# u's products in blocks of four token tiles, with two more x tiles kept in DRAM

## The chip, the cores and the metric

The kernel runs on one core of one Trainium2 chip. Its engines are TensorE (matmuls, in the profile PE, its weight loads PEld), VectorE (DVE), ScalarE (ACT), GpSimd (POOL) and SyncE (SP), which here only issues DMAs. The metric is the device time of one execution in microseconds, from the first to the last instruction with what lies around them.

## The reference

Two branches work on the same x (2048 tokens, 640 features) and are mixed by a gate:

```
g = sigmoid(sum(x * gate_w))                       # one value per token
a = x @ dre.T ;  b = x @ dim.T ;  y = sre @ a - sim @ b     # Fourier mixing, 2048x2048 and 640x640
q = x @ w_q ; s1 = q[..:128] @ k1.T ; s2 = q[128..] @ k2.T  # 32 heads, 16 + 16 scores each
top 2 of s1, top 2 of s2 -> 4 sums -> top 2 of them -> softmax weights gg, expert numbers e
act = gelu(x @ u[e]) ;  B = sum(gg * act * v[e])            # 256 experts
out = g * y + (1 - g) * B
```

As there are only 256 experts, the kernel computes gelu(x @ u.T) for all of them (u's products, the part that the change touches), builds the sparse matrix of weights per token, and multiplies by v.

## The kernel before, in words

Every float32 operand is split into a high and a low part (h is a rounded copy, made by ScalarE; l = f - h, by GpSimd or VectorE), and a product takes three matmuls: h by h, h by l, l by h (`mm3`, lines 143 to 145). Lines 138 and 139 are the split for every operand, so in the profile its groups are told apart by tile names.

The work is written out as one static order. The sequence transform has 128 *pieces* (`seq_piece`): for w in (re, im), for four column blocks c of 512 time steps, for 16 token tiles s of 128: five groups of three matmuls of 512 columns into banks 0 to 4 of PSUM. A column block (16 pieces) is called q; when it ends, ScalarE copies the five banks to the stage ST (line 246), VectorE multiplies by the gate (line 217) and ScalarE's queue stores the five results to DRAM (`store_piece`, line 227). A piece's own operand is loaded five pieces ahead (SP's queue) and split three pieces ahead.

`at(n, f)` hangs other work behind piece n; it is issued, in the order in which it was hung there, after that piece's matmuls:

- Pieces 0 to 29: x is loaded and split into 16 tiles X0 to X15. The query weights are folded with the keys: 32 tiles `wq` of 640 KB are loaded by SP, five in flight, and multiplied in eight groups G of 32 small matmuls (`w_part`, line 365), behind pieces 6, 9, ... 27. `make_t` and `split_w` turn the results into the score weights WH, WL and their sums TW, which lie in the place of X0 to X5.
- From piece 31, the score phase: eight pairs p of token tiles, four `score_step`s each, one behind each piece. Step 0 computes two products into bank 5, splits the sums of x (`split_sums_xT`, tiles SX), then u's products of the pair (`u_pair`, lines 720 to 731): 30 matmuls with 256 columns into bank 7, a gelu on ScalarE (line 729) and two stores on SP's queue (line 731); then ScalarE copies bank 5 to bank 7 (line 548), on which step 1 goes on. Steps 2 and 3 end the scores of the two tiles, load and split the next pair's x (tiles xh and xl, one pair each) and form its sums on VectorE (`sum_xT`, lines 437 to 440). Behind every odd pair but the last stands one piece without a step, a *filler*.
- The Pump (`bg`) hands out VectorE's picking of the top 2 (`topk`, `gates`, `weights`) and the expert matrices in small portions: each `run_bg(us)` behind a group of matmuls adds 0.95 times its time as credit, each portion issued takes its estimate from it. It also issues the copies of rows (line 697) on ScalarE by timers, 5 us apart.
- Then pieces 66 to 127 with the expert matrices (line 815) among them, and 84 steps that multiply by the hidden transform and v. Raw tiles for these steps are taken from places that have come free (`raw_tags`, `take`).

X0 to X8 have to make room in the score phase: they are stored to DRAM early (`put_x`, 9 tiles, `AWAY`), loaded again for each column block into the places of X6, X7 and X8 (`get_x`), and put back in their own places after piece 66 (N1).

All DMAs of one queue are issued in order; SP's issue waits when its operand or its place isn't ready, and what stands behind waits too.

Of the kernel before, what the change touches and what calls it, by code (L numbers as in the profile page):

```python
# [38 lines left out]
KZ = KD + 1  # L39
NSTEP = 7 * KZ  # L40
AHEAD = 5
AWAY = 9
BYPASS = 4
ACCUM_END = NT * (NC + 2) - 4

# [61 lines left out]
def gated_mix_kernel(ctx: ExitStack, tc: tile.TileContext, xT, xn, dreT, dimT, wsre, wsim, wq, kT, uT, vv, gw, out):  # L107
# [20 lines left out]
    def ps_t(shape, dt=F32):  # L128
        return bank(7, shape, dt)
# [6 lines left out]
    def split(f, h, l, eng):  # L136

        nc.scalar.activation(h, f, AF.Copy)  # L138
        eng.tensor_sub(l, f, h.bitcast(F32))  # L139
# [56 lines left out]
    def at(n, f, *args):  # L196
        then.setdefault(n, []).append(lambda: f(*args))
# [51 lines left out]
    for q in range(2 * NC):  # L249
        n = NT * (q + 1)  # L250
        at(n + (2 if q == 0 else -2 if q > 1 else -1), load_row, q)
        at(n + (7 if q == 0 else 0), gate_piece, q)
        if q in (1, 2, 3, 4):
            for d in range(KD):
                at(n + 1 + d, store_piece, q, (d,))
        else:
            at(n + (8 if q == 0 else 1), store_piece, q)


    p1_stack = ctx.enter_context(ExitStack())  # L260
    p1 = p1_stack.enter_context(tc.tile_pool(name="p1", bufs=1, reuse_waits="tile"))
    pools = [p1]

    def load_x(s):
        if s < NT:
# [4 lines left out]
    def split_x(s):  # L270

        if s < NT:
            X[s] = big.tile([P, 2, D], F32R, name="X", tag=f"X{s}")
            f = xr[s // 2][:, s % 2]
            if s:
                split(f, X[s][:, 0], X[s][:, 1], nc.vector)
                return
            psp[0] = h, l = WS[:, 0, 0], WS[:, 0, 1]
            a, b, w = slice(0, 2 * P), slice(2 * P, D), pf.pop(0)
            nc.vector.tensor_copy(X[0][:, 0, a], f[:, a])  # L280
            nc.scalar.activation(h, w, AF.Copy)
            nc.scalar.activation(X[0][:, 0, b], f[:, b], AF.Copy)
            nc.vector.tensor_sub(l, w, h.bitcast(F32))
            for c in (a, b):
                nc.vector.tensor_sub(X[0][:, 1, c], f[:, c], X[0][:, 0, c].bitcast(F32))
# [20 lines left out]


    warm = nc.const_aps.tensor(1.0, [P, 2 * P], mybir.dt.bfloat16)
    t = ps_t([P, 2 * P])
    for n in range(WARM):  # L310
        nc.tensor.matmul(t, warm[:, :P], warm, start=True, stop=True)  # L311

    split_x(0)
    load_piece(4)
# [105 lines left out]
    def split_xT(p, n):  # L420

        if p < NP:
            if not xs:
                xs.update((t, big.tile([P, 2, KD, P], F32R, name=t, tag=t)) for t in ("xh", "xl"))
            split(xf[p][:, n], xs["xh"][:, n], xs["xl"][:, n], nc.gpsimd)

    SX = {}

# [21 lines left out]
        nc.sync.dma_start(xd[s], X[s].bitcast(F32))  # L450

    def get_x(s, tag):
        X[s] = big.tile([P, 2, D], F32R, name="X", tag=f"X{tag}")
        nc.sync.dma_start(X[s].bitcast(F32), xd[s])

    for s in range(AWAY):
        at(6 + 2 * s, put_x, s)
    for s in range(3):
        at(2 * NT - 5 + s, get_x, s, 6 + s)
    for n in range(NT - 4):  # L460
        at(n, load_x, n + 4)
    for n in range(NT - 3):
# [6 lines left out]
    for G in range(NG):  # L469
        b = 6 + 3 * G  # L470
        for m in range(4 * G, 4 * G + 4):
            at(b, w_part, m)
        at(b, split_w, G)
        if G >= NG // 2:
            at(b + (4, 3, 2, 1)[G - NG // 2], make_t, G)
        for i, m in enumerate(range(4 * G + WQB, 4 * G + WQB + 4)):
            at(b + i // 2, load_wq, m)
    n = b + 2
    at(n - 8, load_xT, 0)
    for k in range(KD):  # L480
        at(n - 8 + k, load_u, k)
        at(n - 6 + k, split_u, k)
    for a in range(2):
        at(n - 3, split_xT, 0, a)
    at(n - 1, sum_xT, 0)
    assert N0 == n + 1

# [34 lines left out]
    def products(o, *terms, first=False):  # L522


        terms = [t for a, w in terms for t in zip(*a, *w)]
        for n, (ah, al, wh, wl) in enumerate(terms):
            mm3(o, ah, al, wh, wl, first and n == 0, n == len(terms) - 1, True)
            run_bg(0.68)

    def x_part(n, k0, k1):  # L530
        return [[xs[t][:, n, k] for k in range(k0, k1)] for t in ("xh", "xl")]

    def s_part(n):
        return [[t[:, k * P:(k + 1) * P] for k in range(2)] for t in SX[n]]
# [9 lines left out]
    def score_step(p, a):  # L544


        i0, i1 = 2 * p, 2 * p + 1
        copy = lambda o, f: nc.scalar.activation(o, f, AF.Copy)  # L548
        if a == 0:
            AB["A"] = bank(5)  # L550
            products(AB["A"], (x_part(0, 0, 2), w_part2(0, 2, 0)), first=True)
            split_sums_xT(p)
            u_pair(p)
            AB["Z"] = bank(7)
            copy(AB["Z"], AB["A"])
        elif a == 1:
            products(AB["Z"], (x_part(0, 2, 4), w_part2(2, 4, 0)), (x_part(0, 4, 5), w_part2(4, 5, 0)))
            new_sc(i0)
            copy(sc_half(i0, 0), AB["Z"])
            AB["Y"] = bank(6)  # L560
            products(AB["Y"], (s_part(1), t_part(1)), first=True)
            AB["Z"] = bank(7)
            copy(AB["Z"], AB["Y"])
            load_xT(p + 1)
        elif a == 2:
            products(AB["A"], (s_part(2), t_part(2)))
            copy(sc_half(i0, 1), AB["A"])
            products(AB["Z"], (s_part(4), w_part2(2, 4, 1)), (x_part(0, 4, 5), w_part2(4, 5, 1)))
            nc.vector.tensor_add(sc_half(i0, 1), sc_half(i0, 1), AB["Z"])
            bg.credit -= 0.75  # L570
            picks(i0, scs.pop(i0))
            products(AB["A"], (s_part(3), t_part(3)))
            new_sc(i1)
            copy(sc_half(i1, 1), AB["A"])
            split_xT(p + 1, 0)
        else:
            products(AB["Y"], (x_part(1, 4, 5), w_part2(4, 5, 1)))
            nc.vector.tensor_add(sc_half(i1, 1), sc_half(i1, 1), AB["Y"])
            products(AB["A"], (x_part(1, 2, 4), t_part(4)), (x_part(1, 4, 5), w_part2(4, 5, 0)))
            copy(sc_half(i1, 0), AB["A"])  # L580
            bg.credit -= 0.75
            picks(i1, scs.pop(i1))
            split_xT(p + 1, 1)
            sum_xT(p + 1)
# [132 lines left out]
        if i % NB == NB - 1:  # L717
            bg.add(gates(i // NB))

    def u_pair(p):  # L720
        xh, xl = xs["xh"], xs["xl"]
        ps = bank(7, (P, 2, 2 * P))
        for n in range(2):
            c = slice(n * P, (n + 1) * P)
            for k in range(KD):
                mm3(ps[:, n, :], UH[:, k, c], UL[:, k, c], xh[:, :, k, :], xl[:, :, k, :], k == 0 and n == 0, k == KD - 1, True)
            run_bg(1.8)
        act = p2.tile([P, 2, 2 * P], F32, name="act")
        nc.scalar.activation(act, ps, AF.Gelu_apprx_tanh)
        for n in range(2):  # L730
            nc.sync.dma_start(actd[n][:, 2 * p * P:2 * (p + 1) * P], act[:, n])

    for p in range(NP):
        n = N0 + 4 * p + p // 2
        for a in range(4):
            at(n + 1 + a, score_step, p, a)
    N1 = n + 5
# [3 lines left out]
            at(n - (3 if s > 2 else 5), get_x, s, 6 + s % 3)  # L741
    for s in range(3, AWAY):
        at(N1 - 5 + s, get_x, s, s)
    for s in range(3):
        at(N1 + 6 + 3 * s, get_x, s, s)

# [116 lines left out]
            draw.pop(m)  # L863

    for m in range(2):
        at(N1 + 4 + 2 * m, load_dd, m)
    for m in range(KD):
        for a in range(2):
            at(N1 + 6 + 5 * m + 2 * a, split_dd, m, a)
# [44 lines left out]
    def split_sums(k):  # L914
        if k == KD:
            f = p3.tile([P, 4 * TC], F32R, name="ts", tag="hot0")
            TS[8] = f[:, :2 * D]
            raw_free.append(f[:, 2 * D:2 * D + TC].bitcast(F32))
            raw_tags.extend((("xf", 2), ("X9", 2)))
        for n in () if k == KD else [k] + ([5 + k // 2] if k % 2 == 0 else []):  # L920
            TS[n] = big.tile([P, 2 * D], F32R, name="ts", tag=f"X{(1, 3, 4, 5, 6, 0, 2, 7)[n]}")
        t = T["t"]
        t1, t5, t3, t6 = (t[:, n * 2 * P:(n + 1) * 2 * P] for n in range(4))
        for n, f in enumerate((t1, t3, t5, t6, t[:, 8 * P:])):
            split(f, t_sum(k, n, 0), t_sum(k, n, 1), nc.gpsimd if n < 2 else nc.vector)
        bg.credit -= 1.0

    def load_v():
        T[KD] = big.tile([P, 2, D], F32, name="dt", tag="X9")
        nc.sync.dma_start(T[KD], vv.rearrange("k p d -> p k d"))  # L930

    def split_v():
# [13 lines left out]
    at(NPC + 14, store_gates, 1)  # L946


    fresh, raw_free = deque(), deque()
    raw_tags = [("X8", 2)] + [("wf", 1)] * 4 + [("X10", 2), ("wf", 1)] + [(f"X{s}", 2) for s in range(11, 16)]  # L950
    raw, sp = {}, {}

    def take(key):
# [305 lines left out]
```

## Time and profile before

| | before |
|---|---|
| median of 3 runs | 753.86 us (752.98 to 754.19) |
| the profiled execution | 753.44 us, span 751.7 us |
| TensorE busy | 746.7 us, 4045 matmuls |
| VectorE busy | 587.4 us |
| ScalarE busy | 361.7 us |
| GpSimd busy | 346.6 us |
| DMA | 165.89 MB, mean 221 GB/s |

A line of the timeline gives the start (us from the span's beginning), the length (us), the engine, the source line, the instruction, what it writes <- what it reads, the shapes where there are any, and how many are merged; in brackets the time that the engine stood idle before it and what ended that. "ACTq" and "SPq" are DMA issues on the engine's queue. A line of the windows gives a stretch, its length, the busy time of PE, PEld, DVE, ACT and POOL with their numbers of instructions, the granted clock, the DMA engines' busy share and GB/s. A line of the waits names who waited for whom: us in total, how often, the longest. A line of the chain that ended last gives start, length and what ran.

### The profile page before, as it was taken

What the parts mean: (1) busy time and instruction counts of PE and PEld (TensorE: products, weight loads), DVE (VectorE), ACT (ScalarE), POOL (GpSimd) and SP (SyncE); (2) the same over time, 40 slices, a digit from 0 to 9 for tenths busy, and PEclk for the clock granted to TensorE, in tenths of its full rate; (3) what the DMA queues carried; (4) which work ended last, traced back from release to release, by engine and by line L of the source; (5) the groups of instructions that cost most, each with busy time, mean ns of one, the idle gap of its engine ahead of it and who ended that gap; (6) DMA issues with size and microseconds to landing.
All of it is one profiled execution on the core that took longest, in us unless ns stands there. A gap on an engine that the chain in (4) does not pass through costs nothing.

```text
span 751.7 us, 11366 instructions
## 1 busy us (share of the span) xinstructions
PE 746.7 (99%) x4045; PEld 610.7 (81%) x4045; DVE 587.4 (78%) x741; ACT 361.7 (48%) x660; POOL 346.6 (46%) x286
## 2 busy tenths in 40 slices
PE   9999999999999999999999999999999999999998
PEld 7777777888888888888888888888888888888887
DVE  6864088278999999998999888979999983357651
ACT  4334134534345835553734687633555653443451
POOL 5533225342424424334345445643356793487253
PEclk9999999999999999999999999999999999999999
DMA  9999999478366786663496856388766689775301
GB/s 334 378 388 356 342 381 345 132 191 278 57 174 149 184 273 164 159 167 118 121 376 210 175 146 203 116 255 291 264 225 209 218 261 335 228 233 182 112 29 71
DMA packets 84490, 165.89 MB, mean 221 GB/s; under 512 B 16081, under 2 KB 23377, under 8 KB 84177
## 3 DMA queue, kind: packets, MB, share of 16 engines
q1 hardware_dynamic: 70960, 140.89, 55.5%
q0 software_dynamic: 5472, 9.96, 8.6%
q10 hardware_dynamic: 8000, 14.31, 5.2%
q8 instruction: 32, 0.52, 0.3%
q14 instruction: 26, 0.20, 0.1%
HBM read 132.46 MB, written 31.08 MB: 218 GB/s over the span
## 4 chain that ended last, share of the span: by engine, by line
PE 96%; DMA 2%; DVE 2%; issue 0%; SPq 0%; ACT 0%
PE b L143 30%; PE b L144 30%; PE b L145 30%; PE b L239 2%; PE b L365 2%; DMA wq<-in_wq 2%; PE b L815 1%; PE b L311 1%; DVE ST L217 1%; DVE WU L139 0%; DVE tw L139 0%; DVE wp L371 0%; ACT WU L138 0%; DVE tt L397 0%; DVE tt L396 0%
## 5 line engine op out<-in xcount | busy, mean ns | idle before, releaser
L143 PE MATMUL b<-WS,X 128*128 128x512 f32 x620 | 243.5, 393 | 0.0
L144 PE MATMUL b<-WS,X 128*128 128x512 f32 x620 | 241.5, 389 | 0.0
L145 PE MATMUL b<-WS,X 128*128 128x512 f32 x620 | 241.3, 389 | 0.0
L139 POOL TENSOR_TENSOR WS<-wf,WS 128x512 fp32r<-128x512 f32 x89 | 135.9, 1532 | 162.8 <-ACT WS L138 157.9
L143 PEld LDWEIGHTS b<-WS,X 128*128 128x128 f32 x620 | 116.4, 188 | 28.0 <-issue 4.1
L145 PEld LDWEIGHTS b<-WS,X 128*128 128x128 f32 x620 | 116.4, 188 | 24.5
L144 PEld LDWEIGHTS b<-WS,X 128*128 128x128 f32 x620 | 116.4, 188 | 23.3
L138 ACT ACTIVATE WS<-wf 128x512 fp32r<-128x512 f32 x89 | 55.7, 629 | 76.9 <-PE b L145 32.1
L803 DVE TENSOR_TENSOR hot<-rows,wtab 128x1024 f16<-128x1024 f16 x64 | 62.7, 1005 | 0.7 <-PE b L815 0.6
L139 POOL TENSOR_TENSOR WS<-ra,WS 128x512 fp32r<-128x512 f32 x39 | 55.1, 1426 | 15.3 <-ACT WS L138 13.2
L139 POOL TENSOR_TENSOR xl<-xf,xh 128x640 fp32r<-128x640 f32 x16 | 28.2, 1767 | 69.3 <-ACT xh L138 62.9
L138 ACT ACTIVATE WS<-ra 128x512 fp32r<-128x512 f32 x55 | 34.5, 631 | 50.9 <-PE b L145 36.0
L548 ACT ACTIVATE sc<-b 128x512 f32<-128x512 f32 x32 | 19.2, 600 | 80.7 <-PE b L145 80.7
L191 POOL DMA_DIRECT2D WS<-in_wsre x30 | 26.4, 880 | 68.0 <-ACT WS L189 66.6
L773 ACT ACTIVATE b<-b,mask 128x128 f32<-128x128 f32 x128 | 43.0, 342 | 13.5 <-PE b L815 10.4
L139 POOL TENSOR_TENSOR WP<-ra,WP 128x512 fp32r<-128x512 f32 x18 | 26.4, 1482 | 43.2 <-ACT WP L138 43.1
L598 DVE TENSOR_TENSOR eq<-sc,mm 128x1024 f16<-128x1024 f32 x32 | 41.4, 1293 | 0.9
L605 DVE TENSOR_REDUCE tied<-eq 128x64 f32<-128x1024 f16 x32 | 39.0, 1219 | 0.9
L596 DVE TENSOR_REDUCE mm<-sc 128x64 f32<-128x1024 f32 x32 | 38.8, 1212 | 0.3
L217 DVE SCALAR_TENSOR_TENSOR ST<-ST,grow 128x512 f32<-128x512 f32 x40 | 31.4, 846 | 0.6 <-ACT ST L246 0.6
L143 PE MATMUL b<-WU,xh 128*128 128x512 f32 x80 | 31.2, 391 | 0.0
L145 PE MATMUL b<-WU,xl 128*128 128x512 f32 x80 | 31.1, 389 | 0.0
(203 smaller groups left out, 1468.8 us busy)
## 6 DMA issues: line engine op xcount, KB each, us to landing
wq<-in_wq SPq DMA_DIRECT2D x32, 640.0 KB, 7.1
X<-xd SPq DMA_DIRECT2D x30, 640.0 KB, 6.6
wf<-in_wsim SPq DMA_DIRECT2D x64, 256.0 KB, 4.8
wf<-in_wsre SPq DMA_DIRECT2D x63, 256.0 KB, 6.5
ra<-pd SPq DMA_DIRECT2D x47, 256.0 KB, 3.7
pd<-ST ACTq DMA_DIRECT2D x35, 256.0 KB, 5.2
WS<-in_wsre POOLq DMA_DIRECT2D x30, 256.0 KB, 5.3
xd<-X SPq DMA_DIRECT2D x9, 640.0 KB, 9.4
```

What stands on the lines that cost most here:

```text
L138: nc.scalar.activation(h, f, AF.Copy)
L139: eng.tensor_sub(l, f, h.bitcast(F32))
L143: nc.tensor.matmul(o, wh, ah, start=first, stop=False, skip_group_check=more)
L144: nc.tensor.matmul(o, wh, al, start=False, stop=False, skip_group_check=more)
L145: nc.tensor.matmul(o, wl, ah, start=False, stop=last, skip_group_check=more)
L191: nc.gpsimd.dma_start(l, (wsre, wsim)[w][c, s], accum_op=OP.add)
L217: nc.vector.scalar_tensor_tensor(f, f, -1.0 if w else 1.0, g, op0=OP.mult, op1=OP.mult)
L596: nc.vector.tensor_reduce(m, sc, op=OP.max, axis=AX.X)
L598: nc.vector.tensor_tensor(eq, sc, m[:, :, None].to_broadcast([P, HH, E]), op=OP.is_equal)
L605: nc.vector.tensor_reduce(tied[:, s, ib, :], eq, op=OP.add, axis=AX.X)
L773: nc.scalar.activation(f[:, :, n], f[:, :, n], AF.Copy, scale=mask4[:, n:n + 1])
L803: nc.vector.tensor_tensor(o, a, b, op=op)
```

## The change

- **u's products.** `u_pairs` replaces `u_pair`. It runs in step 0 of odd pairs only and takes both pairs, so 512 columns: 15 matmuls into bank 7, 15 into bank 6, a gelu on each, and one store of 256 KB behind each gelu, now on ScalarE's queue. The first half's gelu is issued before bank 5's copy to bank 7, the second half's after it. The pump is told 0.68 us per group of three, where it was told 1.8 us per 15.
- **Places.** To keep x of two pairs, xh and xl become tiles of two pairs each. xh takes the places of X9 and X10, xl those of X11 and X12; each two places are now one allocation (`place`, `TWIN`). So X9 and X10 are stored to DRAM too (`AWAY` 11), behind piece 25, and loaded on demand like X0 to X8; X11 and X12 are copied by ScalarE to the old places of xh and xl behind pieces 16 and 17 (`move_x`), and back behind piece 66. The first split of x goes from piece 26 to 27.
- **Stores.** The five stores of q = 0 go from piece 24 to piece 28.
- **Fillers.** They stand behind pairs 0, 2 and 4 instead of 1, 3 and 5.
- **After the score phase.** The loads of the hidden transform for `split_dd` start one and two pieces later; v's tile and the raw tiles are placed anew on the joined places. The last of the 19 warm-up matmuls fills the other half of its bank.

```diff
-AWAY = 9
+AWAY = 11
@@ store_piece
-            at(n + (8 if q == 0 else 1), store_piece, q)
+            at(n + (12 if q == 0 else 1), store_piece, q)
@@ new
+    TWIN = {}
+    def place(tag):
+        if tag in (9, 11):
+            TWIN[tag] = big.tile([P, 2, 2, D], F32R, name="X", tag=f"X{tag}")
+        if tag in (9, 10, 11, 12):
+            return TWIN[tag - (tag + 1) % 2][:, (tag + 1) % 2]
+        return big.tile([P, 2, D], F32R, name="X", tag=f"X{tag}" if isinstance(tag, int) else tag)
+
+    def move_x(s, tag):
+        old, X[s] = X[s], place(tag)
+        nc.scalar.activation(X[s], old.bitcast(F32), AF.Copy)
@@ split_xT
-                xs.update((t, big.tile([P, 2, KD, P], F32R, name=t, tag=t)) for t in ("xh", "xl"))
-            split(xf[p][:, n], xs["xh"][:, n], xs["xl"][:, n], nc.gpsimd)
+                xs.update((t, big.tile([P, 2, 2, KD, P], F32R, name=t, tag=tag)) for t, tag in (("xh", "X9"), ("xl", "X11")))
+            split(xf[p][:, n], xs["xh"][:, p % 2, n], xs["xl"][:, p % 2, n], nc.gpsimd)
@@ schedule of pieces 0 to 29
-    for s in range(AWAY):
+    for s in range(9):
         at(6 + 2 * s, put_x, s)
+    for s, tag in ((11, "xh"), (12, "xl")):
+        at(s + 5, move_x, s, tag)
+    for s in range(9, AWAY):
+        at(b - 2, put_x, s)
-        at(n - 3, split_xT, 0, a)
+        at(n - 2, split_xT, 0, a)
@@ score_step, a == 0
             split_sums_xT(p)
-            u_pair(p)
+            act = u_pairs(p // 2) if p % 2 else lambda: None
             AB["Z"] = bank(7)
             copy(AB["Z"], AB["A"])
+            act()
@@ u's products
-    def u_pair(p):
+    def u_pairs(c):
         xh, xl = xs["xh"], xs["xl"]
-        ps = bank(7, (P, 2, 2 * P))
+        def act(n, ps):
+            f = p2.tile([P, TC], F32, name="act")
+            nc.scalar.activation(f, ps, AF.Gelu_apprx_tanh)
+            nc.scalar.dma_start(actd[n][:, c * TC:(c + 1) * TC], f)
         for n in range(2):
-            c = slice(n * P, (n + 1) * P)
+            e = slice(n * P, (n + 1) * P)
+            ps = bank(7 - n)
             for k in range(KD):
-                mm3(ps[:, n, :], UH[:, k, c], UL[:, k, c], xh[:, :, k, :], xl[:, :, k, :], k == 0 and n == 0, k == KD - 1, True)
-            run_bg(1.8)
-        act = p2.tile([P, 2, 2 * P], F32, name="act")
-        nc.scalar.activation(act, ps, AF.Gelu_apprx_tanh)
-        for n in range(2):
-            nc.sync.dma_start(actd[n][:, 2 * p * P:2 * (p + 1) * P], act[:, n])
+                mm3(ps, UH[:, k, e], UL[:, k, e], xh[:, :, :, k, :], xl[:, :, :, k, :], k == 0, k == KD - 1)
+                run_bg(0.68)
+            if n == 0:
+                act(n, ps)
+        return lambda: act(1, ps)
 
     for p in range(NP):
-        n = N0 + 4 * p + p // 2
+        n = N0 + 4 * p + min((p + 1) // 2, 3)
@@ after the score phase
+    for s in (11, 12):
+        at(N1, move_x, s, s)
-        at(N1 + 4 + 2 * m, load_dd, m)
+        at(N1 + 5 + 3 * m, load_dd, m)
```

More of the change, by code (lines that the diff above doesn't have):

```diff
@@ L272, in split_x @@
         if s < NT:
-            X[s] = big.tile([P, 2, D], F32R, name="X", tag=f"X{s}")
+            X[s] = place(s)
             f = xr[s // 2][:, s % 2]
@@ L308, in gated_mix_kernel @@
     warm = nc.const_aps.tensor(1.0, [P, 2 * P], mybir.dt.bfloat16)
-    t = ps_t([P, 2 * P])
+    t = ps_t([P, TC])
     for n in range(WARM):
-        nc.tensor.matmul(t, warm[:, :P], warm, start=True, stop=True)
+        c = slice(0, 2 * P) if n < WARM - 1 else slice(2 * P, TC)
+        nc.tensor.matmul(t[:, c], warm[:, :P], warm, start=n < WARM - 1, stop=True, skip_group_check=n == WARM - 1)
     split_x(0)
@@ L452, in get_x @@
     def get_x(s, tag):
-        X[s] = big.tile([P, 2, D], F32R, name="X", tag=f"X{tag}")
+        X[s] = place(tag)
         nc.sync.dma_start(X[s].bitcast(F32), xd[s])
-    for s in range(AWAY):
+    for s in range(9):
         at(6 + 2 * s, put_x, s)
@@ L528, in products, with x_part @@
             run_bg(0.68)
-    def x_part(n, k0, k1):
-        return [[xs[t][:, n, k] for k in range(k0, k1)] for t in ("xh", "xl")]
+    def x_part(p, n, k0, k1):
+        return [[xs[t][:, p % 2, n, k] for k in range(k0, k1)] for t in ("xh", "xl")]
     def s_part(n):
@@ L550, in score_step @@
             AB["A"] = bank(5)
-            products(AB["A"], (x_part(0, 0, 2), w_part2(0, 2, 0)), first=True)
+            products(AB["A"], (x_part(p, 0, 0, 2), w_part2(0, 2, 0)), first=True)
             split_sums_xT(p)
-            u_pair(p)
+            act = u_pairs(p // 2) if p % 2 else lambda: None
             AB["Z"] = bank(7)
             copy(AB["Z"], AB["A"])
+            act()
         elif a == 1:
-            products(AB["Z"], (x_part(0, 2, 4), w_part2(2, 4, 0)), (x_part(0, 4, 5), w_part2(4, 5, 0)))
+            products(AB["Z"], (x_part(p, 0, 2, 4), w_part2(2, 4, 0)), (x_part(p, 0, 4, 5), w_part2(4, 5, 0)))
             new_sc(i0)
@@ L567, in score_step @@
             copy(sc_half(i0, 1), AB["A"])
-            products(AB["Z"], (s_part(4), w_part2(2, 4, 1)), (x_part(0, 4, 5), w_part2(4, 5, 1)))
+            products(AB["Z"], (s_part(4), w_part2(2, 4, 1)), (x_part(p, 0, 4, 5), w_part2(4, 5, 1)))
             nc.vector.tensor_add(sc_half(i0, 1), sc_half(i0, 1), AB["Z"])
@@ L576, in score_step @@
         else:
-            products(AB["Y"], (x_part(1, 4, 5), w_part2(4, 5, 1)))
+            products(AB["Y"], (x_part(p, 1, 4, 5), w_part2(4, 5, 1)))
             nc.vector.tensor_add(sc_half(i1, 1), sc_half(i1, 1), AB["Y"])
-            products(AB["A"], (x_part(1, 2, 4), t_part(4)), (x_part(1, 4, 5), w_part2(4, 5, 0)))
+            products(AB["A"], (x_part(p, 1, 2, 4), t_part(4)), (x_part(p, 1, 4, 5), w_part2(4, 5, 0)))
             copy(sc_half(i1, 0), AB["A"])
@@ L917, in split_sums @@
             TS[8] = f[:, :2 * D]
-            raw_free.append(f[:, 2 * D:2 * D + TC].bitcast(F32))
-            raw_tags.extend((("xf", 2), ("X9", 2)))
+            raw_free.extend(LENT[0][:, a * TC:(a + 1) * TC] for a in range(2))
+            raw_tags.append(("xf", 2))
         for n in () if k == KD else [k] + ([5 + k // 2] if k % 2 == 0 else []):
@@ L928, in load_v @@
     def load_v():
-        T[KD] = big.tile([P, 2, D], F32, name="dt", tag="X9")
+        f = big.tile([P, 2, 2, D], F32, name="dt", tag="X9")
+        T[KD], f = f[:, 0], f[:, 1].rearrange("p k d -> p (k d)")
+        fresh.extend(f[:, a * TC:(a + 1) * TC] for a in range(2))
+        LENT.append(T[KD].rearrange("p k d -> p (k d)"))
         nc.sync.dma_start(T[KD], vv.rearrange("k p d -> p k d"))
@@ L946, in gated_mix_kernel @@
     at(NPC + 14, store_gates, 1)
-    fresh, raw_free = deque(), deque()
-    raw_tags = [("X8", 2)] + [("wf", 1)] * 4 + [("X10", 2), ("wf", 1)] + [(f"X{s}", 2) for s in range(11, 16)]
+    LENT, fresh, raw_free = [], deque(), deque()
+    raw_tags = [("X8", 2)] + [("wf", 1)] * 5 + [("X11", 5)] + [(f"X{s}", 2) for s in range(13, 16)]
     raw, sp = {}, {}
```

## The prediction

> **What bounds the kernel now.** I read the page first (busy time, granted clock, the chain that ended last), then TensorE's timeline, then the timelines of ScalarE and VectorE where a pair of token tiles ends.
>
> ```profile
> PE 746.7 (99%) x4045; PEld 610.7 (81%) x4045; DVE 587.4 (78%) x741; ACT 361.7 (48%) x660; POOL 346.6 (46%) x286
> PEclk9999999999999999999999999999999999999999
> PE 96%; DMA 2%; DVE 2%; issue 0%; SPq 0%; ACT 0%
> ```
>
> TensorE is the bound from end to end, at its full granted clock. So time can only be won by fewer or cheaper matmuls, or in the few gaps between them. A matmul's busy time doesn't tell its price, because successive matmuls overlap; the distance from start to start does. TensorE's timeline around u's products of pair 0, and at the kernel's end, where the moving operand is a plain row of 256:
>
> ```profile
> 136.95 0.28 PE L143 MATMUL b<-xh,WU 128*128 128x256 f32 x1
> 140.54 0.40 PE L143 MATMUL b<-WS,X 128*128 128x512 f32 x1
> 143.97 0.39 PE L143 MATMUL b<-WU,xh 128*128 128x512 f32 x1
> 147.37 0.39 PE L143 MATMUL b<-WS,X 128*128 128x512 f32 x1
> 150.77 0.39 PE L143 MATMUL b<-tw 128*128 128x512 f32 x1
> ...
> 743.88 0.28 PE L143 MATMUL b<-WP,ts 128*128 128x256 f32 x1
> 748.07 0.28 PE L145 MATMUL b<-WS,ts 128*128 128x256 f32 x1
> ```
>
> The 30 matmuls of u take 140.54 - 136.95 = 3.59 us, 119.7 ns each. Fifteen matmuls of 512 columns (147.37 to 150.77) take 3.40 us, 226.7 ns each. Twice 119.7 is 239.4: halving the width costs 12.7 ns a matmul. That isn't the broken-up operand of u (two stretches of 128): at the end 35 matmuls on plain rows take 4.19 us, 119.7 ns again.
>
> **The change part by part.** (1) *u in 512 columns.* Eight blocks of 30 matmuls become four of 30: 240 x 119.7 = 28.72 us goes, 120 x 226.7 = 27.20 us comes: -1.52. The piece right behind a narrow block takes 143.97 - 140.54 = 3.43 us instead of 3.40; behind wide matmuls it has no cause to: 8 x 0.03 = -0.24. Bounds: four stretches of 128 might cost something two don't, then the gain is 0; more than 1.76 there isn't.
>
> [...]
>
> (2) *The stores of q = 0 (the first column block's results) go from piece 24 to piece 28; x tiles 9 and 10 are stored at piece 25.* TensorE's only real gaps are at the keys' products (line 365). The chain in order of time, TensorE's timeline, ScalarE's and SP's queue:
>
> ```profile
> 80.21 2.29 PE b L365 x32
> ```
> ```profile
> 105.56 1.82 PE L365 MATMUL b<-wq,kp 128*32 128x320 f32 x24
> ...
> 108.28 0.50 PE L143 MATMUL b<-WS,X 128*128 128x512 f32 x1
> ...
> 118.72 1.82 PE L365 MATMUL b<-wq,kp 128*32 128x320 f32 x24
> 121.17 0.74 PE L365 MATMUL b<-wq,kp 128*32 128x320 f32 x8 [0.63 <-DMA wq<-in_wq]
> 121.85 0.50 PE L143 MATMUL b<-WS,X 128*128 128x512 f32 x1
> ```
> ```profile
> 104.64 3.93 ACTq L227 DMA_DIRECT2D pd<-ST  x5
> ```
> ```profile
> 114.24 0.63 SPq L356 DMA_DIRECT2D wq<-in_wq  x1
> ```
>
> A group of 32 takes 2.29 us; the last two take 108.28 - 105.56 = 2.72 and 121.85 - 118.72 = 3.13: 0.43 + 0.84 = 1.27 us of waiting for wq. Just ahead of the second wait ScalarE's queue issues 5 x 256 KB of stores. At piece 28 they come when the last wq tile has been used. The two stores of 640 KB that take their place stand behind wq's last load (114.24) in SP's queue. Bounds 0 and 1.27; I take -1.05, all of the second wait and half of the first, whose tile was loading before the stores began. What the new places cost: the stores block ScalarE for up to 3.93 us at piece 28 instead. Behind them stand make_t's splits and pair 0's sums; pair 0's copy into bank 7 moves to about 138.2 (four splits of 128x256, then the copy), wanted at 135.59 + 1.36 + 3.40 = 140.4: hidden, 2.2 us to spare, and 1.7 us is lost if the full block comes on top. The first split of x now also waits for tiles 9 and 10 to be stored; pieces are split three ahead, some 10 us.
>
> (3) *Steps and fillers.* In an even pair u's 3.59 us goes and a filler piece of 3.40 follows the pair; in an odd pair u takes 6.80 and the filler behind it goes. Pair to pair that is 29.3 and 32.7 us where 29.5 and 32.9 were, so VectorE's share of work per pair stays (its pacing counts 27.2 us for u where it counted 28.8):
>
> ```profile
> 227.40:260.20 32.80, 32.80 (x160) 27.78 (x159) 30.55 (x34) 22.57 (x33) 12.22 (x12) 1.00 0.71 167
> 260.20:289.70 29.50, 29.50 (x146) 25.01 (x145) 28.85 (x45) 13.77 (x24) 10.70 (x11) 1.00 0.84 254
> 378.40:420.00 41.60, 41.60 (x185) 34.47 (x184) 40.71 (x53) 17.62 (x24) 21.14 (x15) 1.00 0.90 295
> ```
>
> But between an odd pair's end and the next even pair's second step the cover shrinks. That step's first matmul needs line 548's copy into bank 7, which stands on ScalarE behind the splits of x's sums. From the pair's last matmul TensorE has one piece, six matmuls, one piece: 3.40 + 1.36 + 3.40 = **8.16 us**, where it had 15.2. The chain now, by the first matmul after pairs 1, 3, 5 and 6, VectorE's first sum (line 437), and ScalarE:
>
> ```profile
> 191.11 0.39 PE L143 MATMUL b<-WS,X 128*128 128x512 f32 x1
> 253.43 0.39 PE L143 MATMUL b<-WS,X 128*128 128x512 f32 x1
> 315.75 0.39 PE L143 MATMUL b<-WS,X 128*128 128x512 f32 x1
> 348.61 0.39 PE L143 MATMUL b<-WS,X 128*128 128x512 f32 x1
> ...
> 360.52 0.50 PE L143 MATMUL b<-WU,xh 128*128 128x512 f32 x1
> ```
> ```profile
> 194.22 0.43 DVE L437 TENSOR_TENSOR xf<-xf 128x256 f32<-128x256 f32 x1 [1.03 <-POOL xl L139]
> 256.92 0.43 DVE L437 TENSOR_TENSOR xf<-xf 128x256 f32<-128x256 f32 x1 [1.41 <-POOL xl L139]
> 318.85 0.43 DVE L437 TENSOR_TENSOR xf<-xf 128x256 f32<-128x256 f32 x1 [1.02 <-POOL xl L139]
> 354.91 0.42 DVE L437 TENSOR_TENSOR xf<-xf 128x256 f32<-128x256 f32 x1
> ```
> ```profile
> 196.52 0.71 ACT L138 ACTIVATE h<-xf 128x256 fp32r<-128x256 f32 x2
> 259.25 1.94 ACT L697 ACTIVATE rows<-rt 128x384 f16<-128x384 f16 x1
> 261.61 0.71 ACT L138 ACTIVATE h<-xf 128x256 fp32r<-128x256 f32 x2
> 322.90 0.72 ACT L138 ACTIVATE h<-xf 128x256 fp32r<-128x256 f32 x2
> 323.51 1.97 ACT L697 ACTIVATE rows<-rt 128x384 f16<-128x384 f16 x1
> 357.22 0.72 ACT L138 ACTIVATE h<-xf 128x256 fp32r<-128x256 f32 x2 [0.46 <-DVE xf L440]
> 359.89 0.58 ACT L548 ACTIVATE b<-b 128x512 f32<-128x512 f32 x1
> ```
>
> With 0.6 us for the copy, it would end at 197.83, 262.9 and 324.2 for pairs 2, 4 and 6: 6.7, 9.5 and 8.5 us after the pair's end. Pair 2 fits. Pairs 4 and 6 are late by 1.3 and 0.3 as ScalarE stands, since one or two copies of rows (line 697) go first. These come at 5 us intervals by the pump's clock, and the splits are now issued 3.4 us of TensorE's time sooner, so the fourth copy of rows falls behind them. Without it pair 4 would be about 2.5 us earlier. Bounds 0 and 1.6; I take +0.3. In odd pairs the cover grows to 18 us (15 for pair 7), and pair 7's present wait goes: its second step starts at 360.52, right behind the copy (359.89 + 0.58), 360.52 - 348.61 = 11.91 us after the pair's end where 3.40 + 1.36 + 3.59 + 3.43 = 11.78 were due, and a further 0.16 is lost in its first matmuls: -0.29.
>
> (4) *Hidden.* Six more loads of x (36 for 30) and two more stores, and u's results on ScalarE's queue:
>
> ```profile
> X<-xd SPq DMA_DIRECT2D x30, 640.0 KB, 6.6
> ```
> ```profile
> SPq L731 <- ACT act L729: 86.8, 8, 21.3
> ```
>
> The tightest stretch is 378 to 420, at 295 GB/s; two loads more make it (12.3 + 1.3 MB) / 41.6 us = 327. Loads go out three pieces (10.2 us) ahead and land in 6.6; cost 0, some 2 us if they slip by half. SP's queue no longer stands 86.8 us behind the gelu; its transfers weren't late for TensorE, so that's worth 0. The gelu's store on ScalarE delays what follows by 0.4 us, in odd pairs only. The four copies that move tiles 11 and 12 take some 1.3 us each (my estimate, from 0.63 us for 512 columns and 0.74 for 640), at pieces 16, 17 and 66 where ScalarE is idle over half the time. Near piece 122 v's load must wait for one x tile more, 3.4 us; it goes out after that already.
>
> **Sum:** 753.44 (the profiled execution: span 751.7) - 1.52 - 0.24 - 1.05 - 0.29 + 0.30 = 750.64, that is -2.80. The median of the runs is 0.42 above the profiled one; from it the sum would be 751.06. I put 751.0.
>
> **The rivals.**
> - *wq's waits stay.* Its loads queue behind x's tiles and pieces too, and the first wait began with a load issued ahead of the stores. Then 753.86 - 1.75 = about 752.1. For it: the DMA engines are full here with or without the stores. Against: 1.3 MB less ahead of the last load is over 3 us, more than the 0.84 that it lacked. Chance 0.17.
> - *The copies of rows stay ahead of bank 7's copy* in pairs 4 and 6, the fourth too (323.51 + 1.97 + 0.6 = 326.1, 10.3 after the pair): 1.3 + 2.2 = 3.5 us, the gain is gone: 753.9. Chance 0.13.
> - *Slower: VectorE arrives late in the even pairs.* In pair 7 it didn't wait for anything before the sums; it was behind, and began 354.91 - 348.61 = 6.3 us after the pair's end, against 3.1, 3.5 and 3.1 in pairs 2, 4 and 6. From its start to the copy's end it takes 3.6 us, so from 4.6 us on TensorE waits; at 6.3 it's 1.7 us in each of the three pairs, and 753.86 - 3.1 + 5.1 = 755.9. It turns the balance from a mean lateness of 1.0 us. Against: gates and weights, which make VectorE late, still come in even pairs and hit odd ones. Chance 0.10.
> - *Four stretches of 128 cost what two matmuls did:* u brings 0, 752.5. Chance 0.05, as the end's plain rows show no price for two.
>
> **How the numbers follow.** The forecast has the remaining 0.55: 751.0, its own range 750.1 to 752.2 (wq 0 to 1.27, bank 7 0 to 1.6). A measurement here can tell about 0.2%, 1.5 us. Faster by more (below 752.35): all of the forecast, 0.12 of the first rival, 0.03 of the rest: 0.70. Slower: 0.10. Within: 0.20. The range for 8 in 10 goes from 749.7 (everything won, 753.86 - 3.32, less the 0.9 us by which the lowest run stood under the median) to 753.9.
>
> **What would show it.** Right: u's matmuls 226 to 228 ns apart, four blocks of 6.8 us; the last two groups of line 365 at 2.3 us; no wait of TensorE at the second step of pairs 2, 4 and 6. Wrong: 240 ns there; 3.1 us for the last group; line 548's copy ending within 0.1 us of that step's first matmul, with line 697 or a late line 437 ahead of it; or a new wait of TensorE on an X tile after 380 us or on VectorE's hot tiles near the end.

## The result, and the profile after

The changed kernel takes 758.49 us, the median of six runs (756.62 to 760.36); the kernel before, on the same chip, 753.51 (752.22 to 754.30). The ratio is 1.0065, with a 95% interval of 1.0046 to 1.0085: **slower by 5 us**, where 751.0 was forecast. The profiled execution took 757.09 us (span 755.2), 3.65 more than the one of before.

The page of the changed kernel, its engines and the chain that ended last:

```profile
PE 745.7 (99%) x3925; PEld 603.5 (80%) x3925; DVE 588.6 (78%) x741; ACT 365.2 (48%) x664; POOL 344.3 (46%) x286
PE 67%; issue 12%; DVE 10%; POOL 6%; DMA 3%; SPq 1%; ACT 0%; POOLq 0%; ACTq 0%; DVEq 0%
```

There are 120 matmuls fewer, as meant. But the chain, 96% TensorE before, is 67% TensorE now: somewhere TensorE waits for others. Its timeline, at the keys' products and then in pair 3 and pair 7, shows the gains and the losses side by side:

```profile
105.06 2.36 PE L380 MATMUL b<-wq,kp 128*32 128x320 f32 x32
117.77 2.36 PE L380 MATMUL b<-wq,kp 128*32 128x320 f32 x32
...
226.27 0.39 PE L143 MATMUL b<-xh,WU 128*128 128x512 f32 x1
233.07 0.39 PE L143 MATMUL b<-WS,X 128*128 128x512 f32 x1
236.25 0.39 PE L145 MATMUL b<-WS,X 128*128 128x512 f32 x1
237.64 0.50 PE L143 MATMUL b<-WU,xh 128*128 128x512 f32 x1 [1.00 <-ACT b L567]
247.97 0.39 PE L145 MATMUL b<-WU,xl 128*128 128x512 f32 x1
250.48 0.50 PE L143 MATMUL b<-tw,h 128*128 128x512 f32 x1 [2.12 <-ACT sc L567]
...
350.61 0.39 PE L143 MATMUL b<-xh,WU 128*128 128x512 f32 x1
360.59 0.39 PE L145 MATMUL b<-WS,X 128*128 128x512 f32 x1
362.88 0.50 PE L143 MATMUL b<-WU,xh 128*128 128x512 f32 x1 [1.91 <-ACT b L567]
```

What was won: both groups of the keys' products (line 380 now) run as 32 matmuls in one row, with no wait between 24 and 8 of them; u's block takes 233.07 - 226.27 = 6.80 us for 30 matmuls, 226.7 ns each. What was lost: between two starts that are normally 0.23 us apart lie 1.39, 2.51 and 2.29 us, so TensorE stands for 1.16, 2.28 and 2.06 us. With the slower matmuls right behind each stop, the pieces and steps there take 4.0 us more than their matmuls need in pair 3, and 2.8 in pair 7. In pairs 1 and 5 TensorE has no such stop.

All three stops end with a copy by ScalarE (line 567; it was 548). ScalarE's timeline in pairs 3, 5 and 7, and SP's queue in pairs 3 and 7 (its last row is pair 7's):

```profile
229.87 0.60 ACT L747 ACTIVATE act<-b 128x512 f32<-128x512 f32 x1 [1.21 <-PE b L145]
236.62 0.34 ACTq L748 DMA_DIRECT2D actd<-act  x1
237.01 0.58 ACT L567 ACTIVATE b<-b 128x512 f32<-128x512 f32 x1 [6.53 <-DMA X<-xd]
239.25 0.60 ACT L747 ACTIVATE act<-b 128x512 f32<-128x512 f32 x1 [1.66 <-DMA actd<-act]
241.82 0.33 ACTq L748 DMA_DIRECT2D actd<-act  x1
242.19 0.63 ACT L188 ACTIVATE WS<-wf 128x512 fp32r<-128x512 f32 x1 [2.34 <-DMA xf<-in_xT]
...
248.08 1.93 ACT L717 ACTIVATE rows<-rt 128x384 f16<-128x384 f16 x1
249.47 0.96 ACT L567 ACTIVATE sc<-b 128x512 f32<-128x512 f32 x1
...
299.13 0.60 ACT L747 ACTIVATE act<-b 128x512 f32<-128x512 f32 x1 [1.82 <-PE b L145]
305.67 0.33 ACTq L748 DMA_DIRECT2D actd<-act  x1
...
354.75 0.72 ACT L138 ACTIVATE h<-xf 128x256 fp32r<-128x256 f32 x2 [0.46 <-DVE xf L455]
356.78 0.60 ACT L747 ACTIVATE act<-b 128x512 f32<-128x512 f32 x1
361.85 0.35 ACTq L748 DMA_DIRECT2D actd<-act  x1
362.25 0.58 ACT L567 ACTIVATE b<-b 128x512 f32<-128x512 f32 x1 [4.87 <-DMA rt<-gs]
```
```profile
232.20 0.57 SPq L469 DMA_DIRECT2D X<-xd  x1
...
237.52 1.00 SPq L433 DMA_DIRECT2D xf<-in_xT  x2
...
359.58 1.09 SPq L712 DMA_TRANSPOSE rt<-gs  x1
```

The gelu of pair 3 ends at 230.47, but its store goes out only at 236.62: ScalarE stands still for 6.15 us, and with it the copy that TensorE's next step needs. In pair 7 it's 4.47 us (357.38 to 361.85). The brackets name what ended the wait, and it's nothing that has to do with the store: **an X tile, a load of x (xf) and a transpose of the experts' weights (rt<-gs), all three on SP's queue.** How long those took from issue to landing, in the view of the DMA issues around each:

```profile
X<-xd SPq DMA_DIRECT2D x1, 640.0 KB, 4.3
...
xf<-in_xT SPq DMA_DIRECT2D x1, 320.0 KB, 4.2
...
rt<-gs SPq DMA_TRANSPOSE x1, 2.2
```

232.20 + 4.3 = 236.5, 237.52 + 4.2 = 241.7 and 359.58 + 2.2 = 361.8: ScalarE's three stores go out at 236.62, 241.82 and 361.85, each within 0.1 us of such a landing. In pair 5 the second store is held too, for 5.94 us (299.73 to 305.67), until an X tile has landed; no stop of TensorE follows there.

That 4.47 us cost more in pair 7 than 6.15 in pair 3 has to do with VectorE. In pair 7 its sums of x come late, ScalarE's splits wait for them (the bracket at 354.75), and the gelu ends 6.77 us after u's block begins (350.61), where in pair 3 it ends after 4.20. So ScalarE had 6.15 - 1.16 = 5.0 us of cover in pair 3 and 4.47 - 2.06 = 2.4 in pair 7.

Why these? The trace records which semaphore each DMA raises (in 16 steps, the last of them the landing) and for which one an engine waits. In the changed kernel's trace SP's 459 DMAs and ScalarE's 60 share eight semaphores (100, 102 to 105 and 108 to 110), and GpSimd's 38 have eight others (111 to 118). In the list in which the built program has the DMAs of both queues, the eight follow each other in one order that repeats over all 519. So a DMA's semaphore was last used by the DMA **eight places before it in that list**, and of the 511 that have one there, none went out in this trace before that one had landed. Counted in the list: eight places before the first store of pair 3 stands the load of X, eight before the second a half of xf, eight before the first store of pair 7 the transpose of gs.

The trace shows the wait itself: just ahead of the stores at 236.62, 241.82, 305.67 and 361.85 ScalarE waits for the very semaphore that the store then raises (100, 109, 100 and 100), and the DMA that used it before had landed at 236.54 (X), 241.74 (xf), 305.60 (X) and 361.77 (gs). In eight of the traces, those of the two kernels and of e1, e3, e4, e7, e8 and e9 below, none of 4088 DMAs of the two queues (511 in each) went out before its semaphore's previous user had landed.

In the experiments this is **theory O** (the order decides). In a first form, **theory L**, I had only that a store on ScalarE's queue waits for loads of SP's. The rivals: **S**, VectorE's sums are late; **B**, the single buffer `act` makes the second gelu wait; **B2**, that single buffer on ScalarE's queue; **P**, a gate row loaded one piece later is the cure; **Q**, the queue hurts only with the new tiling.

### The profile page after: what moved, and what is told of

The parts are those of the page before. It is cut to its first block, busy times and chain, and to the rows that moved or that the text cites. A ratio compares the mean times of both kernels' runs of the same rounds, so it can differ in the third digit from the quotient of the medians.

```text
span 755.2 us, 11144 instructions
## 1 busy us (share of the span) xinstructions
PE 745.7 (99%) x3925; PEld 603.5 (80%) x3925; DVE 588.6 (78%) x741; ACT 365.2 (48%) x664; POOL 344.3 (46%) x286
## 4 chain that ended last, share of the span: by engine, by line
PE 67%; issue 12%; DVE 10%; POOL 6%; DMA 3%; SPq 1%; ACT 0%; POOLq 0%; ACTq 0%; DVEq 0%
PE b L143 21%; PE b L144 20%; PE b L145 20%; PE b L380 2%; PE b L239 2%; POOL xl L139 2%; POOL WS L191 2%; DVE eq L618 1%; DVE tied L625 1%; POOL WS L139 1%; PE b L844 1%; DVE mm L616 1%; DMA WS<-in_wsim 1%; DMA actd<-act 1%; DVE eq L623 1%
## 5 line engine op out<-in xcount | busy, mean ns | idle before, releaser
L139 POOL TENSOR_TENSOR xl<-xf,xh 128x640 fp32r<-128x640 f32 x16 | 26.5, 1660 | 70.7 <-ACT xh L138 70.7
L832 DVE TENSOR_TENSOR hot<-rows,wtab 128x1024 f16<-128x1024 f16 x64 | 54.4, 876 | 2.5 <-PE b L844 2.5
L139 POOL TENSOR_TENSOR WS<-ra,WS 128x512 fp32r<-128x512 f32 x33 | 47.4, 1447 | 14.8 <-ACT WS L138 14.6
L138 ACT ACTIVATE WS<-ra 128x512 fp32r<-128x512 f32 x47 | 29.4, 631 | 42.8 <-PE b L145 29.9
L618 DVE TENSOR_TENSOR eq<-sc,mm 128x1024 f16<-128x1024 f32 x32 | 43.9, 1371 | 0.9
L217 DVE SCALAR_TENSOR_TENSOR ST<-ST,grow 128x512 f32<-128x512 f32 x40 | 33.2, 893 | 1.5 <-DMA grow<-gdr 1.5
L139 POOL TENSOR_TENSOR WP<-ra,WP 128x512 fp32r<-128x512 f32 x13 | 19.2, 1489 | 31.0 <-ACT WP L138 30.9
L832 DVE TENSOR_TENSOR hot<-hot,rows 128x1024 f16<-128x1024 f16 x32 | 33.1, 1036 | 0.0
```

Of the source, the lines that this page charges most:

```text
L217: nc.vector.scalar_tensor_tensor(f, f, -1.0 if w else 1.0, g, op0=OP.mult, op1=OP.mult)
L618: nc.vector.tensor_tensor(eq, sc, m[:, :, None].to_broadcast([P, HH, E]), op=OP.is_equal)
L832: nc.vector.tensor_tensor(o, a, b, op=op)
```

## The experiments

### The stores on another queue, and a second buffer

Four versions of the changed kernel; e1 has one of the two edits, e3 the other, e2 and e5 both.

```diff
 e1: the stores on SP's queue
-            nc.scalar.dma_start(actd[n][:, c * TC:(c + 1) * TC], f)
+            nc.sync.dma_start(actd[n][:, c * TC:(c + 1) * TC], f)
 e3: a second buffer for the second gelu, in the place of a gate row
-            f = p2.tile([P, TC], F32, name="act")
+            f = p2.tile([P, TC], F32, name="act", tag=("act", "grow")[n])
 ... which is loaded one piece later for it
-        at(n + (2 if q == 0 else -2 if q > 1 else -1), load_row, q)
+        at(n + (2 if q == 0 else -2 if q > 1 and q != 3 else -1), load_row, q)
 e2: both edits, nc.sync        e5: both edits, nc.gpsimd
```

> The changed kernel, but u's results are stored on SP's queue again; one buffer for the gelu's result, as in the change. Theory L (the store on ScalarE's queue has to wait until an SP load issued some DMAs before it has landed, and that load stands behind the loads of rows which wait for VectorE's weights; so ScalarE stands still 6.1 us in pair 3 and 4.4 us in pair 7): ScalarE is free for bank 7's copy, so the first stall of each of these pairs goes (1.2 + 0.4 and 2.1 + 0.6 us), but the second gelu still waits for the first result's store to land, now behind the same loads on SP's queue, which keeps ScalarE late in pair 3: 752 to 754. Rival S (VectorE's sums come too late in pairs 3 and 7): as the changed kernel, 757 to 759. Rival B (only the one buffer matters): 756 to 758.

> The changed kernel, with u's results stored on SP's queue and the second half's gelu in a buffer of its own (the gate row's place; the gate row of q = 3 is loaded one piece later). Theory L: nothing holds ScalarE back in pairs 3 and 7 any more, TensorE has no gap over 0.5 us between 130 and 380, and the predicted gains stay: 750 to 751.5. Rival S: 757 to 759. Rival B: 750 to 751.5.

> The changed kernel with two buffers for the gelu, the stores still on ScalarE's queue. Theory L: the first store still waits for the SP load, so bank 7's copy comes as late as in the changed kernel (TensorE waits 1.2 us in pair 3 and 2.1 us in pair 7); the second gelu is then no longer held up, which wins 1 to 2 us: 755 to 757. Rival S: 757 to 759. Rival B: 750 to 751.5.

> The changed kernel with two buffers, the stores on GpSimd's queue, whose DMAs don't take turns with SP's and ScalarE's. Theory L: no stall of ScalarE; a store takes GpSimd about 0.9 us (line 191's row), four pairs times two; GpSimd is idle there: 750 to 752. Rival S: 757 to 759. Rival B: 750 to 752.

Beside a kernel before of 754.25 us: e1 750.45 (ratio 0.9950, interval 0.9937 to 0.9964), e2 750.55 (0.9952, 0.9939 to 0.9964), e3 750.20 (0.9947, 0.9934 to 0.9959), e5 750.15 (0.9948, 0.9936 to 0.9961). All four are faster than both kernels, by some 4 us and some 8 us, and TensorE has no stop over 0.4 us anywhere in the score phase. S falls as a cause by itself, as VectorE's sums are as late in all of them as in the changed kernel: in pair 7 the last one begins 3.2 us after u's block. B falls in the same way: e1 has a single buffer and loses nothing. That is also better than its expected 752 to 754, as its second gelu isn't held up in pair 3. But e3 was a miss for theory L: the stores are still on ScalarE's queue, and nothing is lost. ScalarE's timeline of e3:

```profile
230.95 0.60 ACT L747 ACTIVATE act<-b 128x512 f32<-128x512 f32 x1 [1.20 <-PE b L145]
231.58 0.33 ACTq L748 DMA_DIRECT2D actd<-act  x1
```

The store goes out 0.03 us after its gelu. In the built list of e3 the first store of pair 3 stands six places earlier, ahead of the gate row, three transposes and xf's two loads; eight places before it is then a raw tile that had landed (at 211.22). Only in pair 5 is e3's second store held, for 5.9 us and without a stop of TensorE, as in the changed kernel. That made theory O of theory L: not the queue alone, but the place in the order. But e3 also has a second buffer and a later gate row, either of which might be the cure, so the next runs change one thing each.

### The place in the order, with queue and buffer as they are

```diff
 e7: the gates' weights are let in later; the transposes of gs and rp follow them
-        bg.after(4.0, lambda: bg.q[0].appendleft(weights(b, c, rp, gs)))
+        bg.after(4.0 if b == NT // NB - 1 else 10.0, lambda: ...)
 e8: the later gate row of e3 alone
-        at(n + (2 if q == 0 else -2 if q > 1 else -1), load_row, q)
+        at(n + (2 if q == 0 else -2 if q > 1 and q != 3 else -1), load_row, q)
 e9: the first step of those transposes later
-            bg.space(lambda a=a: step(a), 5.0 if a else 16.0 if b == NT // NB - 1 else 8.0)
+            bg.space(lambda a=a: step(a), 5.0 if a else 16.0 if b == NT // NB - 1 else 16.0)
```

> The changed kernel, its one buffer act and ScalarE's queue kept; only the gates' weights (L689 to L697 of the changed kernel) are let in 10 us instead of 4 us of background time after their exponential, in all batches but the last. In the order of the program the stores of pairs 3 and 7 then stand ahead of rt<-gs, so the DMA that used a store's completion semaphore before is one that landed long before. Theory O (a store on ScalarE's queue waits until the DMA eight places before it in the program's order, SP's and ScalarE's counted together, has landed): ScalarE issues both stores within 0.5 us of their gelu, and no step of pairs 3 and 7 has a gap of TensorE over 0.5 us behind them: 750 to 752 us. Rival B2 (one buffer on ScalarE's queue is the cause, wherever the store stands): the second gelu is held as before, 756 to 759 us. Rival P (e3 was cured because the gate row of q=3 came later): 756 to 759 us. Against theory O would be a late X tile that comes out of SP's queue behind rt<-gs, 6 us later than now: up to 2 us more.

> The changed kernel with the other half of e3 alone: the gate row of q=3 is loaded one piece later, the buffer act stays single and the stores stay on ScalarE's queue. In the program's order the four odd pairs' stores stand where they stood. Theory O: nothing changes, the first store of pair 3 goes out some 6 us after its gelu, that of pair 7 some 5 us after: 757 to 760 us. Rival P (the later gate row was what cured e3): 750 to 752 us.

> The changed kernel; only the first step of the gate rows (L712's transposes) is spaced by 16.0 instead of 8.0. By the program's order the store of pair 7 then has an X tile of long before eight places ahead, the store of pair 3 the same rt<-gs that follows VectorE's weights (231.03 us in the changed kernel), with no X tile between. Theory O, a dose: no hold in pair 7 (2.8 us of TensorE's time back), in pair 3 a hold of 2 to 4 us in place of 5.1 us, 1 to 3 us of gaps in place of 4.0: 752.5 to 755.5 us. Rival B2: as the changed kernel, 756.5 to 759.5. Rival P: as the changed kernel too.

Beside a kernel before of 753.68 us: e7 750.78 us (ratio 0.9962, interval 0.9948 to 0.9977), e8 762.29 (1.0109, 1.0089 to 1.0129), e9 751.52 (0.9965, 0.9953 to 0.9977). **Theory O holds, B2 and P fall.** ScalarE's timelines, of e7 and e8 and e9 in this order:

```profile
231.19 0.60 ACT L747 ACTIVATE act<-b 128x512 f32<-128x512 f32 x1 [1.21 <-PE b L145]
231.81 0.33 ACTq L748 DMA_DIRECT2D actd<-act  x1
```
```profile
357.26 0.60 ACT L747 ACTIVATE act<-b 128x512 f32<-128x512 f32 x1
365.00 0.33 ACTq L748 DMA_DIRECT2D actd<-act  x1
365.37 0.58 ACT L567 ACTIVATE b<-b 128x512 f32<-128x512 f32 x1 [7.51 <-DMA grow<-gdr]
```
```profile
230.81 0.60 ACT L747 ACTIVATE act<-b 128x512 f32<-128x512 f32 x1 [1.21 <-PE b L145]
235.77 0.33 ACTq L748 DMA_DIRECT2D actd<-act  x1
236.15 0.58 ACT L567 ACTIVATE b<-b 128x512 f32<-128x512 f32 x1 [4.74 <-DMA rt<-gs]
```

In e7 the DMA eight places before, a raw tile's load, had landed at 211.26, and the store goes out at once. In e9 it's rt<-gs, as counted beforehand, and the store waits for it. In e8 pair 7 waits longer than expected, 7.1 us where "some 5" stood: the gate row had moved behind rt<-gs in the list and become the eighth itself. The time, 762.3, missed the expected 757 to 760 mostly by that: of the 5.3 us between the two profiled executions some 3.6 are pair 7's, and 1.3 are a longer wait of TensorE for an operand's load at 428 us, which I have not traced. Six different kinds of DMA have thus ended the wait of a store (an X tile, xf, gs, a gate row, and in e4 below rp and a raw tile), each the one that the count names.

e9 came out better than the 752.5 to 755.5 expected: a hold of 4.36 us (231.41 to 235.77) in pair 3 stopped TensorE nowhere in the score phase. That fits the 5.0 us of cover that 6.15 us and a stop of 1.16 gave for this pair.

### The queue alone, in the kernel before

```diff
 e4: the kernel before
-            nc.sync.dma_start(actd[n][:, 2 * p * P:2 * (p + 1) * P], act[:, n])
+            nc.scalar.dma_start(actd[n][:, 2 * p * P:2 * (p + 1) * P], act[:, n])
```

> The kernel before with one thing changed: its u stores (L731) go out on ScalarE's queue. In its program's order the DMA eight places before the first store of pair 3 is rt<-rp of the second row step, which SP issued at 235.93 and which landed at 242.58 in the trace of before, while the gelu ends at 234.04. Theory O: ScalarE stands for 6 to 8 us from 234 on, with its bank copies behind it, and TensorE loses 2 to 5 us there; the other pairs' stores have landed DMAs eight before them: 755.5 to 759 us. Rival Q (ScalarE's queue hurts only together with the new tiling, its single narrow buffer and its two gelus per pair): 753 to 754.5 us, as before.

771.13 us beside 753.68: ratio 1.0228, interval 1.0210 to 1.0246. **Q falls**: one word in a line costs 17 us with the old tiling. The size missed its range by far. ScalarE's timeline, TensorE's, and TensorE's windows around a second stop:

```profile
233.79 0.60 ACT L729 ACTIVATE act<-b 128x512 f32<-128x512 f32 x1
236.42 5.18 ACTq L731 DMA_DIRECT2D actd<-act  x2
241.64 0.58 ACT L548 ACTIVATE b<-b 128x512 f32<-128x512 f32 x1 [7.25 <-DMA actd<-act]
```
```profile
242.28 0.80 PE L143 MATMUL b<-WU,xh 128*128 128x512 f32 x1 [6.00 <-ACT b L548]
...
312.15 0.50 PE L143 MATMUL b<-WU,xh 128*128 128x512 f32 x1 [4.69 <-ACT b L548]
313.17 0.63 PE L143 MATMUL b<-WU,xh 128*128 128x512 f32 x1
313.60 0.63 PE L144 MATMUL b<-WU,xh 128*128 128x512 f32 x1
...
316.14 0.39 PE L144 MATMUL b<-tw 128*128 128x512 f32 x1
```
```profile
300.00:307.50 7.50, 7.47 (x47) 6.44 (x46) 7.23 (x12) 3.02 (x5) 3.14 (x4) 1.00 0.75 187
312.15:315.70 3.55, 3.55 (x9) 2.80 (x10) 3.48 (x4) 1.12 (x2) 0.89 (x1) 0.58 0.29 68
```

The hold of pair 3 was as counted: the first store waits for rt<-rp, the second for a load of X, and ScalarE stands from 234.39 to 241.60. What I hadn't counted were a second stop of TensorE, 4.69 us at 312, where the eighth DMA was a raw tile's load; one of 1.01 us in pair 7, where no store is held but the two issues put off bank 7's copy by 1.0 us, and the kernel before has no cover there; and what follows a long stop. The matmuls behind it start 0.43 us apart (313.17 to 313.60) instead of 0.23, and the granted clock in that stretch is 0.58 where it was 1.00. From 312.15 to 316.14 ten matmuls take 3.99 us where 2.27 are due: the stop costs 1.7 us again after it has ended, that in pair 3 2.7 us (thirteen matmuls). Counted from start to start, the three stops are 6.2, 4.8 and 1.2 us; with 4.4 of slow matmuls that is 16.6, and the remaining 0.9 of the span's 17.5 I have not traced.

### The other parts of the change, one by one

```diff
 e10: the kernel before, the first quarter's stores at piece 28
-            at(n + (8 if q == 0 else 1), store_piece, q)
+            at(n + (12 if q == 0 else 1), store_piece, q)
 e11: e1, those stores back at piece 24
-            at(n + (12 if q == 0 else 1), store_piece, q)
+            at(n + (8 if q == 0 else 1), store_piece, q)
```

> The kernel before with one part of the change alone: x tiles 9 and 10 stay as they are, but the first quarter's stores (q = 0) come at piece 28 instead of 24, behind wq's loads. If the prediction's third term holds (the two waits of L365's groups, 0.43 and 0.84 us, are there because those stores stand ahead of wq's loads), both groups run in about 2.29 us without a wait: 1.0 to 1.3 us less than before, ratio 0.9983 to 0.9987, 752.2 to 753.0 beside a kernel before of 753.5 to 754. If the waits have another cause: as before, ratio 0.9995 to 1.0005.

> The kernel e1 (all of the change, its u stores on SP's queue) with the first quarter's stores back at piece 24: what stays is the tiling of u by four tiles and the filler pieces by even pairs. The prediction's terms for these two are 1.52 + 0.24 + 0.29 = 2.05 us less than before, with 0.30 against it: 1.75 us, so 751.7 to 752.2 beside 753.7, ratio 0.997 to 0.9985. If the stores' place did nothing: as e1, ratio 0.995.

Beside a kernel before of 753.77 us: e10 752.69 (ratio 0.9985, interval 0.9976 to 0.9994), e11 752.47 (0.9984, 0.9972 to 0.9996), twelve runs each. The keys' products in e10 and in e11:

```profile
107.75 0.75 PE L365 MATMUL b<-wq,kp 128*32 128x320 f32 x8 [0.65 <-DMA wq<-in_wq]
118.84 2.36 PE L365 MATMUL b<-wq,kp 128*32 128x320 f32 x32
```
```profile
106.84 0.75 PE L380 MATMUL b<-wq,kp 128*32 128x320 f32 x8 [0.24 <-DMA wq<-in_wq]
121.14 0.75 PE L380 MATMUL b<-wq,kp 128*32 128x320 f32 x8 [1.38 <-DMA wq<-in_wq]
```

The stores' place alone brings 1.1 us, and it's the second wait that goes with it; with the stores back at piece 24 it is back. Of the nine traces with the stores at piece 28, seven don't have the second wait and two (e7, e8) have under 0.3 us of it; the three with the stores at 24 have 0.46 to 1.38. So the second wait has the cause that the prediction named. For the first this isn't shown: at piece 28 it is gone in six traces, but 0.21 to 0.65 us in e1, e3 and e10, at 24 it is 0.22 to 0.74. The new tiling with its fillers brings 1.3 us by itself, somewhat under the 1.75 of the sum, which the interval still holds (0.9977); in e11's trace the second wait is 0.75 us longer than in that of before, which may be part of what is missing.

## Why the prediction was wrong

Step by step, as the prediction put it:

- **(1) u in 512 columns, -1.52 and -0.24:** right. Every block takes 6.80 us, and the piece behind it 3.40.
- **(2) the stores at piece 28, -1.05:** right for the second wait (0.84). That e10 has 1.08 alone bears the sum out in size (0.5 to 1.8 by its interval), not the half of the first wait that was in it, which e10's trace still has; that in the profiled execution of the whole change both were gone (1.27) is partly luck.
- **(3) pair 7's old wait, -0.29, and the late copy in pairs 4 and 6, +0.30:** the first came true wherever ScalarE isn't held; the second didn't appear, as the second steps of pairs 2, 4 and 6 start without a wait.
- **(4) "Hidden": wrong.** "The gelu's store on ScalarE delays what follows by 0.4 us, in odd pairs only" was the term that failed. It counted the issue's own length and not what the issue waits for. The first store held ScalarE for 6.15 us in pair 3 and 4.47 in pair 7, the second of pair 3 for 1.97 more (239.85 to 241.82), that of pair 5 for 5.94, and of these 18.5 us 6.7 reached TensorE, none of it in pair 5. The trace of before shows this wait on ScalarE, small and far from u's products:

```profile
445.40 0.93 ACT L138 ACTIVATE WS<-wf 128x512 fp32r<-128x512 f32 x1
447.15 0.34 ACTq L227 DMA_DIRECT2D pd<-ST  x1
447.54 0.74 ACT L138 ACTIVATE DD<-draw 128x640 fp32r<-128x640 f32 x1 [1.21 <-DMA wf<-in_wsim]
```

A store of a column block's results stands 0.82 us (446.33 to 447.15) until a raw tile's load, which SP issued at 441.47 and which used the same semaphore, has landed at 447.07. So the wait could have been found, and its bound was in reach: SP's rows of before between 234 and 242 were full of transfers (twelve issues, from 234.06 to 242.18).

The account closes nearly: -1.52 - 0.24 - 1.27 - 0.29 = -3.32 and +6.7 make +3.4, where the two profiled executions differ by 3.65; TensorE also stands 0.5 us at 422.8, for an operand's load. And with the hold gone, e1, e2, e3, e5 and e7 take 750.15 to 750.78 us, inside the range that the forecast had for itself (750.1 to 752.2).

None of the rivals was it. "Slower: VectorE arrives late" had the right sign, and a wrong mechanism: the loss comes in the odd pairs, not the even ones, and by a queue. VectorE's lateness has a share in it only in pair 7, where it took 2.6 us of the cover. That rival's price per pair (1.7 us) was even too small, since a held ScalarE is late twice in a pair: for bank 7's copy and, with five result copies and a copy of rows queued up, for the score's copy at 249.47. Only the words that SP's 86.8 us behind the gelu were "worth 0" held in a narrow sense: e1, which puts that wait back on SP's queue, is no slower than e5 (750.45 us beside 750.15). SP has nothing behind its waits that TensorE misses; ScalarE has. The sum of another rival, the copies of rows, has a slip: 753.86 - 3.10 + 3.5 is 754.3, not 753.9.

That e7's cure is the order and not the moment of some transfer rests on the semaphores in the traces: each held store waits for its own semaphore's previous user, and in e7 that user is another one. No run shifted a semaphore and nothing else.

## What to carry to other kernels

The price of a DMA issue on a compute engine was here not its length (0.34 us) but the longest thing that it had to wait for, its semaphore's previous user included (6.15 us in pair 3); everything queued on that engine stood behind it. So in a program built like this one, look up which DMA stands eight places before it in the built order, and put stores of late results on a queue whose engine has nothing urgent (here SP or GpSimd: 750.45 us in e1, 750.15 in e5), or see to it that the eighth DMA is old (750.78 in e7). When a change moves a DMA, time the move by itself: here it turned a gain of 3 to 4 us into a loss of 5.

## What the hardware did that I had not expected

The slow matmuls after a long stop. By the brackets, TensorE stood idle for 4.55 us in e8 (pair 7) and for 4.69 and 6.00 us in e4, and after that the matmuls ran at 0.43 us each for the next 3.4 to 5.6 us, at a granted clock of 0.57 (e8, 366.00 to 369.50), 0.58 (e4, 312.15 to 315.70) and 0.50 (e4, 242.30 to 246.00). After the 1.00, 1.91 and 2.12 us in the changed kernel they didn't: from the second or third matmul on they were 0.23 to 0.24 us apart, and the granted clock is 1.00. So the three stops of up to 2.12 us were followed by no such row of slow matmuls, and the three from 4.55 us on were, which cost 1.7 to 2.7 us on top. What a stop of a length between these does, and what lowers the clock, no run here shows.

And that the issuing engine matters so much, which by these traces is the built program's doing: the wait is one for a semaphore that the program hands out. In e4, where the engine that issues the stores is all that changed, it cost 17 us (771.13 beside 753.68).
